# Decode attention plus bilinear GLU: q made as two rows and spread by matmuls with ones, last w_down loads regrouped

## The chip, the cores and the metric

One core of a Trainium2 chip. The metric is device time in microseconds. The kernel before took 377.58 us (median of 3 runs, 377.46 to 377.84).

## What is computed

Two tokens (B = 2), one layer, in float32: the input is normalised, then x + attention(xn) + GLU(xn) is returned.

```python
# D = 512, H = 32 heads of DH = 128, window W = 2048 of SK = 8192 keys, F = 1376
xn = layernorm(x)
q = xn @ wq                                    # 2 x 4096
k, v = k_cache[:, :, SK-W:], v_cache[:, :, SK-W:]   # 2 x 32 x 2048 x 128 each
scores = einsum("bhqd,bhkd->bhqk", q, k) * DH**-0.5
o = einsum("bhqk,bhkd->bhqd", softmax(scores), v)
h = (xn @ w_gate) * (xn @ w_up)
out = x + o.reshape(B, 1, H*DH) @ wo + h @ w_down
```

Every key and value is used once, so the kernel reads some 159 MB to make 1024 numbers.

## The kernel before

The host lays all weights and the used part of the caches out as one stream, in the order in which the kernel wants them; `loads()` lists it. The 32 heads form 11 groups, `GROUPS`, of three heads (the last has two). The stream is cut into steps. A step is one load on the SP queue into one of three big buffers, `step0` to `step2` (13824 floats on each of 128 partitions), or for a few small ones into `extra`. Odd steps bring the keys of a group together with `wq` for the group after it; even steps bring the values and `wo`. Step n goes into the buffer that step n - 3 left, so its issue waits until the readers of that step are through. The last steps are cut small: the values of the last two heads, `wo` for them, and the pieces 2 to 9 of `w_down` (`wd`, each 128 x 512, 256 KB; NFC = 10). Pieces 2 to 9 are three loads on their own.

For a group g:

- `project(g)` makes q on TensorE. `xnb` holds each value of xn repeated over 128 columns, so each of the 8 matmuls (2 tokens by 4 chunks of D) gives q of a token on all 128 partitions at once, in PSUM, in `q_ps[g % 2]`. It is called for g + 1 while VectorE works on group g, behind the first `products` of the group.
- `products(h)` multiplies the keys of a head in place by q on VectorE, reading q from PSUM; `sums(h)` adds over the head dimension. `maxima(g)`, `weights(g)` and `denominators(g)` make the softmax, with the exponentials on ScalarE.
- `weigh(h)` is the product with the values on TensorE; `fold(g)` copies its result to SBUF on ScalarE, `gather(g)` collects it on TensorE and scales it on VectorE into `oT`; `wo(g, ...)` multiplies by wo.

`project_gu`, `gate` and `turn` make the GLU's hidden layer `hT` early. `down(c, ...)` multiplies piece c of w_down. At the end everything is added up in `acc_g`, four column groups of 32 partitions, by `add_groups`, with four matmuls for a piece. VectorE copies `acc_g` to `o_out` and SP stores it.

Each engine runs its instructions in the order in which the program writes them; `Program.emit` sets semaphores between engines and on loads. The order at the end of the program, after the last `fold`, is: `down` of pieces 2 to 4, `gather`, `down` of 5 to 7, `wo`, `down` of 8 and 9, the copy, the store. Nearly all instructions are recorded by the helper in `Engine.__getattr__` and `Program.put`, so in the profile they all carry line 175, and groups are told apart by the names of their tiles. A float32 matmul of the program shows as two matmul and two weight-load instructions.

Of the kernel before, what the change touches and what calls it, by code (L numbers as in the profile page):

```python
# [10 lines left out]
P = 128  # L11
B, D, H, DH, SK, F = 2, 512, 32, 128, 8192, 1376
# [3 lines left out]
NC = D // P  # L16
FB = 4 * P
NFB = -(-F // FB)
NFC = F // P
# [3 lines left out]
HG = 3  # L23
# [10 lines left out]
def loads():  # L34


    def wq(g):
        return ("wq", g, NC * DH * len(GROUPS[g]))

    def k(h):  # L40
        return ("k", h, CK)

    def v(h):
        return ("v", h, CK)

    def wo(h):
        return ("wo", h, CO)

    def wd(lo, hi):
        return [("wd", i, CO) for i in range(lo, hi)]  # L50

    out = [
        (0, "x", [("c", 0, CX), wq(0)]),
        (1, 0, [k(h) for h in GROUPS[0]] + [wq(1)]),
        (2, 1, [(w, 0, NC * F) for w in ("wg", "wu")]),
        (3, 2, [k(h) for h in GROUPS[1]] + [wq(2)]),
    ]
    turn = (1, 0, 2)
    for g in range(NG - 1):
        n = 4 + 2 * g  # L60
        if g < NG - 2:
            out += [(n, turn[n % 3 - 1], [f(h) for f in (v, wo) for h in GROUPS[g]])]
        if g < NG - 3:
            out += [(n + 1, turn[(n + 1) % 3 - 1], [k(h) for h in GROUPS[g + 2]] + [wq(g + 3)])]
        if g == NG - 3:
            out += [(n + 1, turn[(n + 1) % 3 - 1], [k(h) for h in GROUPS[g + 2]]
                     + wd(0, 2) + [wo(h) for h in GROUPS[g + 1]])]
        if g == NG - 2:
            h = GROUPS[g]
            e, f = GROUPS[g + 1]  # L70
            m = turn[(n + 1) % 3 - 1]
            out += [(n, "x", [v(h[0])]), (n + 1, turn[n % 3 - 1], [v(i) for i in h[1:]]),
                    (n + 2, m, [v(e), wo(e), wo(f)]), (n + 2, m, [v(f)]),
                    (n + 2, m, wd(2, 5)), (n + 2, m, wd(5, 8)),
                    (n + 2, m, wd(8, NFC))]
    return out


# [134 lines left out]
def build(nc, stream, x_nat, wd_rest, out):  # L213
    pr = Program(nc)
    pe, dve, act, pool = pr.pe, pr.dve, pr.act, pr.pool
# [9 lines left out]
    xc = pr.sb("xc", [P, B, NC])  # L225
    sq = pr.sb("sq", [P, B, NC])
    xn = pr.sb("xn", [P, NC, B])
    xnb = pr.sb("xnb", [P, NC * B, P])
    cst = pr.sb("cst", [P, CX])
    p_all = pr.sb("p", [P, 2, HG, B, JG, M])  # L230
    s_t = [pr.sb(f"s{i}", [P, 2 * HG, J]) for i in range(2)]
# [14 lines left out]
    q_ps = [pr.ps(f"q{i}", [P, B, FB]) for i in range(2)]  # L246
# [4 lines left out]
    for n, t, fields in loads():  # L251
        tile = buf_x if t == "x" else buf[t]
        c0 = used.get(n, 0)
        for kind, i, w in fields:
            c = used.get(n, 0)
            got[kind, i] = tile[:, c : c + w]
            used[n] = c + w
        c1 = used[n]
        assert c1 <= tile.shape[1], (n, c1)
        src = stream[pos : pos + P * (c1 - c0)].rearrange("(p i) -> p i", p=P)  # L260
        pos += P * (c1 - c0)
        queue.append((n, tile[:, c0:c1], src))
# [21 lines left out]
    for w in (B * NC, 8 * HG, 8 * HG, 2 * NFB, 2):  # L284
# [5 lines left out]
    id2 = cst[:B, cut[4] : cut[5]]  # L290
# [12 lines left out]
        xn, xc.rearrange("p b c -> p c b"),  # L303
        st[:, 3, :].unsqueeze(1).to_broadcast([P, NC, B]), op=ALU.mult,
    )
    dve.tensor_copy(
        xnb, xn.rearrange("p c b -> p (c b)").unsqueeze(2).to_broadcast([P, NC * B, P])
    )

    def project(g):  # L310
        n = DH * len(GROUPS[g])
        w = got["wq", g].rearrange("p (c n) -> p c n", c=NC)
        for b in range(B):
            for c in range(NC):
                pe.matmul(
                    q_ps[g % 2][:, b, 0:n], xnb[:, c * B + b, :], w[:, c, :],
                    start=(c == 0), stop=(c == NC - 1),
                )

    def keys(h):  # L320
        return got["k", h].rearrange("p (b j d) -> p b j d", b=B, j=J)
# [107 lines left out]
    def down(c, add, **kw):  # L429
        add(hT[:, c % 4, c // 4, :], got["wd", c], **kw)  # L430

    def wo(g, add):
        for hh, h in enumerate(GROUPS[g]):
            add(oT[g % 2][:, B * hh : B * hh + B], got["wo", h])
# [10 lines left out]
    def next_up(g):  # L445
        if g + 1 < NG:
            project(g + 1)
        if g == 0:
            project_gu()
        if g == 1:  # L450
            gate()

    project(0)
    for g in range(NG - 1):
        start_group(g, lambda: next_up(g))
# [14 lines left out]
    g = NG - 1  # L470
# [22 lines left out]
    for c in range(5, 8):  # L493
        down(c, add_groups)
    wo(g, add_groups)
    for c in range(8, NFC):
        down(c, add_groups, last=(c == NFC - 1))
    dve.tensor_copy(o_out, acc_g)
    pr.load("SP", out, o_out)
    pr.emit()  # L500
# [2 lines left out]
def laid_out(x):  # L503
# [33 lines left out]
    def field(kind, i):  # L537
# [13 lines left out]
    parts = [  # L551
        np.concatenate([field(kind, i) for kind, i, _ in fields], axis=1).ravel()
        for _, _, fields in loads()
    ]
    return {"stream": np.concatenate(parts), "x": a, "wd_rest": wd[NFC * P :]}
# [27 lines left out]
```

## Time and profile before

| | |
|---|---|
| median of the runs | 377.58 us |
| the profiled execution | 377.47 us |
| its span | 376.2 us |
| mean granted TensorE clock | 0.773 |

The span runs from the first to the last recorded instruction; the rest of the execution's time lies around it. In the page's lists, "PE" is TensorE, "PEld" its weight loads, "DVE" VectorE, "ACT" ScalarE, "SP" the engine that issues the loads. A row of a list of instructions gives the start, the length, the engine, the line, the operation, output <- inputs, shapes, the count, and in brackets how long the engine stood idle before it and what ended that. A row of groups gives the busy time, the mean in ns, and the idle time before. `q1` is the SP queue of loads, `q8` a queue for instructions.

### The profile page before, as it was taken

To read this page: it belongs to the slowest core of one execution; us is meant where nothing else is said; L and a number is where in the kernel's file an instruction comes from. 1 tells how busy PE (TensorE), PEld (TensorE's weight loads), DVE (VectorE), ACT (ScalarE), POOL (GpSimd) and SP (SyncE) were. 2 spreads that over 40 slices of the span, in tenths; PEclk is the share of its full clock that TensorE was granted. 3 is DMA by queue.
4 is the path that set the end of the run, shared out by engine and by line. 5 is a ranking of instruction groups with operands and counts; after the bars stand their busy time and mean duration, and the time that the engine had idled before them with its cause. 6 is when DMAs were issued, how large, how long until landed. Compare 5 with 4: busy or idle time off the path is not lost.

```text
span 376.2 us, 2481 instructions
## 1 busy us (share of the span) xinstructions
PE 224.2 (60%) x1052; PEld 84.2 (22%) x1052; DVE 298.6 (79%) x159; ACT 29.5 (8%) x143; POOL 1.3 (0%) x5
## 2 busy tenths in 40 slices
PE   1764844769178367616927752691775278088287
PEld 1431122124022112302301230230122023012033
DVE  2069989947995995999499499959949986998950
ACT  2000020020001002000100200010020001001010
POOL 1000000000000000000000000000000000000000
PEclk9968858669586958958685895878689588578879
DMA  9999989999899998999999999999999999999995
GB/s 367 400 459 422 459 388 470 390 453 465 383 460 407 447 459 388 460 429 423 459 394 460 423 423 459 400 455 429 417 459 406 443 438 422 422 439 414 427 426 238
DMA packets 4446, 159.70 MB, mean 425 GB/s; under 512 B 498, under 2 KB 626, under 8 KB 1236
## 3 DMA queue, kind: packets, MB, share of 16 engines
q1 hardware_dynamic: 4320, 159.35, 98.4%
q10 hardware_dynamic: 116, 0.20, 0.2%
q8 instruction: 8, 0.13, 0.1%
q14 instruction: 2, 0.02, 0.0%
HBM read 159.49 MB, written 0.07 MB: 424 GB/s over the span
## 4 chain that ended last, share of the span: by engine, by line
DMA 53%; DVE 36%; PE 9%; SPq 0%; issue 0%
DMA step<-in_stream_dram 53%; DVE s L175 18%; DVE step L175 17%; PE acc L175 5%; PE o_ps L175 2%; PE tr L175 1%; PE q L175 1%; SPq L175 0%; DVE dg L175 0%; DVE mt L175 0%; DVE mtt L175 0%; DVE mc L175 0%; DVE o_sb L175 0%; DVE rec L175 0%; DVE oT L175 0%
## 5 line engine op out<-in xcount | busy, mean ns | idle before, releaser
L175 DVE TENSOR_TENSOR step<-step,q 128x4096 f32<-128x4096 f32 x32 | 141.2, 4414 | 43.6 <-DMA step<-in_stream_dram 43.6
L175 DVE TENSOR_REDUCE s<-step 128x32 f32<-128x4096 f32 x32 | 141.4, 4420 | 0.8
L175 PE MATMUL o_ps<-step,p 128*24 128x512 f32 x496 | 76.8, 782 | 98.0 <-DMA step<-in_stream_dram 98.0
L175 PE MATMUL q<-step,xnb 128*128 128x384 f32 (+1 forms) x160 | 57.6, 517 | 5.4 <-DMA step<-in_stream_dram 5.2
L175 PEld LDWEIGHTS o_ps<-step,p 128*24 128x24 f32 x496 | 16.9, 129 | 154.1 <-DMA step<-in_stream_dram 97.4
L175 PE MATMUL acc<-step,oT 128*2 128x512 f32 x54 | 42.3, 948 | 0.0
L175 PEld LDWEIGHTS q<-step,xnb 128*128 128x128 f32 x160 | 32.2, 206 | 26.0 <-DMA step<-in_stream_dram 6.3
L175 ACT COPY o_sb<-o_ps 128x512 f32<-128x512 f32 x12 | 7.0, 584 | 258.0 <-PE o_ps L175 258.0
L175 ACT ACTIVATE p<-s,nm 128x16 f32<-128x16 f32 x64 | 18.8, 294 | 76.5 <-DVE nm L175 76.5
L175 PE MATMUL tr<-dg,ones 128*128 128x24 f32 (+1 forms) x22 | 5.9, 351 | 23.2 <-DVE dg L175 23.2
L175 PE MATMUL tr<-cst,o_sb 128*128 128x6 f32 (+1 forms) x96 | 12.7, 256 | 7.0 <-ACT o_sb L175 7.0
L175 PEld LDWEIGHTS tr<-cst,o_sb 128*128 128x128 f32 x96 | 11.6, 191 | 17.2 <-ACT o_sb L175 14.9
L175 PE MATMUL o_ps<-step,xn 128*2 128x512 f32 (+1 forms) x48 | 9.9, 741 | 5.0 <-DMA step<-in_stream_dram 5.0
L175 ACT ACTIVATION_READ_ACCUMULATOR p<-s,nm 128x1 f32 x64 | 11.9, 187 | 0.0
L175 PEld LDWEIGHTS acc<-step,oT 128*2 128x2 f32 x54 | 5.2, 108 | 24.3 <-issue 23.9
L175 PEld LDWEIGHTS tr<-dg,ones 128*128 128x128 f32 x22 | 4.6, 261 | 25.8 <-DVE dg L175 24.9
L175 DVE TENSOR_REDUCE nm<-tr 128x6 f32<-128x24 f32 (+1 forms) x11 | 2.0, 183 | 8.5 <-PE tr L175 8.5
L175 PE MATMUL q<-extra,xnb 128*128 128x384 f32 x16 | 7.4, 631 | 1.5 <-DVE xnb L175 1.5
L175 DVE TENSOR_TENSOR oT<-tr,rec 128x6 f32<-128x6 f32 (+1 forms) x11 | 1.7, 157 | 7.0 <-PE tr L175 7.0
L175 PEld LDWEIGHTS tr<-rs,ones 128*128 128x128 f32 x22 | 3.7, 213 | 14.4 <-issue 11.7
L175 PE MATMUL tr<-rs,ones 128*128 128x6 f32 (+1 forms) x22 | 4.7, 286 | 2.4 <-ACT p L175 2.2
L175 PE MATMUL tr<-st,mean_w 128*128 128x2 f32 x4 | 1.2, 363 | 7.2 <-DVE st L175 7.2
(44 smaller groups left out, 40.9 us busy)
## 6 DMA issues: line engine op xcount, KB each, us to landing
step<-in_stream_dram SPq DMA_DIRECT2D x18, 6912.0 KB, 23.0
step<-in_stream_dram SPq DMA_DIRECT2D x1, 6656.0 KB, 33.3
step<-in_stream_dram SPq DMA_DIRECT2D x1, 5504.0 KB, 33.6
step<-in_stream_dram SPq DMA_DIRECT2D x1, 5376.0 KB, 34.3
step<-in_stream_dram SPq DMA_DIRECT2D x1, 4096.0 KB, 26.0
step<-in_stream_dram SPq DMA_DIRECT2D x1, 2560.0 KB, 28.4
extra<-in_stream_dram SPq DMA_DIRECT2D x1, 2048.0 KB, 38.7
step<-in_stream_dram SPq DMA_DIRECT2D x1, 2048.0 KB, 31.6
```

What stands on the lines that cost most here:

```text
L175: ins = getattr(e, method)(*args, **kw)
```

## The change

q of a group is first made as two rows (one for each token) by four matmuls with xn itself as the stationary tile, into the second bank of `q_ps`; ScalarE copies the two rows to SBUF; two matmuls with `one_b`, a 2 x 128 tile with ones in the row of one token, spread each row over the 128 partitions. `xnb` goes, and with it its copy on VectorE; `one_b` is made by a smaller one. The three last loads bring pieces 2 to 4, 5 to 8 and 9 of w_down, in place of 2 to 4, 5 to 7 and 8 to 9.

```diff
@@ loads
-                    (n + 2, m, wd(2, 5)), (n + 2, m, wd(5, 8)),
-                    (n + 2, m, wd(8, NFC))]
+                    (n + 2, m, wd(2, 5)), (n + 2, m, wd(5, 9)),
+                    (n + 2, m, wd(9, NFC))]
@@ build
-    xnb = pr.sb("xnb", [P, NC * B, P])
+    one_b = pr.sb("one_b", [B, B, P])
+    q_sb = [pr.sb(f"q_sb{i}", [B, HG * DH]) for i in range(2)]
...
-    dve.tensor_copy(
-        xnb, xn.rearrange("p c b -> p (c b)").unsqueeze(2).to_broadcast([P, NC * B, P])
-    )
+    dve.tensor_copy(one_b, id2.unsqueeze(2).to_broadcast([B, B, P]))

     def project(g):
         n = DH * len(GROUPS[g])
         w = got["wq", g].rearrange("p (c n) -> p c n", c=NC)
+        q2 = q_ps[g % 2][0:B, B - 1, 0:n]
+        for c in range(NC):
+            pe.matmul(q2, xn[:, c, :], w[:, c, :], start=(c == 0), stop=(c == NC - 1))
+        act.copy(q_sb[g % 2][:, 0:n], q2)
         for b in range(B):
-            for c in range(NC):
-                pe.matmul(
-                    q_ps[g % 2][:, b, 0:n], xnb[:, c * B + b, :], w[:, c, :],
-                    start=(c == 0), stop=(c == NC - 1),
-                )
+            pe.matmul(
+                q_ps[g % 2][:, b, 0:n], one_b[:, b, :], q_sb[g % 2][:, 0:n],
+                start=True, stop=True,
+            )
...
-    for c in range(8, NFC):
-        down(c, add_groups, last=(c == NFC - 1))
+    down(8, add_groups)
+    down(9, add_groups, last=True)
```

The order of the matmuls at the end stays as it was: `down` of 5 to 7, `wo`, `down` of 8, `down` of 9.

## The prediction

> **What bounds the kernel now.** I read the page's busy shares and slices first, then its queues and its chain, then the chain in order of time, then the last ten microseconds instruction by instruction.
>
> ```profile
> PE 224.2 (60%) x1052; PEld 84.2 (22%) x1052; DVE 298.6 (79%) x159; ACT 29.5 (8%) x143; POOL 1.3 (0%) x5
> ...
> DMA  9999989999899998999999999999999999999995
> ...
> q1 hardware_dynamic: 4320, 159.35, 98.4%
> ...
> q8 instruction: 8, 0.13, 0.1%
> ...
> HBM read 159.49 MB, written 0.07 MB: 424 GB/s over the span
> ...
> DMA 53%; DVE 36%; PE 9%; SPq 0%; issue 0%
> ```
>
> The one load queue keeps the 16 DMA engines occupied for 98.4% of the span; no compute engine is above 79%. The chain gives the DMA only 53% because it walks through VectorE wherever a buffer is freed, but the slices show no stretch in which the transfers stand still before the last one. So the end is set by the bytes, by the few microseconds before the first and by those after the last, unless a load is issued so late that the queue runs empty. How far is that?
>
> ```profile
> DMA to landing us min/median/max: 21.1/31.1/49.5
> ...
> 52.00:68.00 16.00, 8.40 (x18) 4.62 (x18) 15.96 (x6) 1.07 (x6) 0.00 (x0) 0.71 1.02 442
> ```
>
> The first row is for all 27 loads into the step buffers, the second a busy stretch whose last column is GB/s. A full load is 6912 KB, 7.08 MB, and takes 16.0 us at 442 GB/s. Even the load with the shortest time from issue to landing, 21.1 us, was therefore issued some 5 us before the transfers ahead of it were through. Nothing starves.
>
> What is left is the tail:
>
> ```profile
> 308.30 21.93 DMA step<-in_stream_dram
> 330.23 0.04 issue
> 330.27 7.61 PE o_ps L175 x48
> 337.89 0.27 SPq L175
> 338.15 0.04 issue
> 338.20 34.10 DMA step<-in_stream_dram
> 372.30 0.04 issue
> 372.34 1.88 PE q L175 x56
> 374.22 0.02 issue
> 374.24 0.29 DVE o_out L175
> ```
>
> ```profile
> 371.23 1.05 PE L175 MATMUL tr<-cst,o_sb 128*128 128x4 f32 x8
> 372.32 0.16 DVE L175 TENSOR_TENSOR oT<-tr,rec 128x4 f32<-128x4 f32 x1 [6.22 <-PE tr L175]
> 372.34 0.84 PE L175 MATMUL q<-step,hT 128*2 128x128 f32 x24
> 372.99 0.62 PE L175 MATMUL q<-step,oT 128*2 128x128 f32 x16
> 373.56 0.33 PEld L175 LDWEIGHTS q<-step,hT 128*2 128x2 f32 x16 [0.24 <-DMA step<-in_stream_dram]
> 373.56 0.62 PE L175 MATMUL q<-step,hT 128*2 128x128 f32 x16
> ```
>
> The first view is the chain (start, length, what), the second the instructions in order of time. The load of pieces 5 to 7 of w_down lands at 372.30; TensorE then does 24 matmul instructions for them, 16 for wo of the last group, waits 0.24 us for pieces 8 and 9, which land about 373.54, does 16 more, and VectorE copies the sums out. From 372.30 to the copy the program is no longer bound by transfers alone but by a landing plus the TensorE work queued behind it.
>
> **The change part by part: q.** Before, project(g) is 8 matmuls over a 128-wide stationary tile; each shows as two instructions.
>
> ```profile
> 22.29 8.01 PE L175 MATMUL q<-step,xnb 128*128 128x384 f32 x16 [5.04 <-DMA step<-in_stream_dram]
> ...
> 151.12 4.81 PEld L175 LDWEIGHTS q<-step,xnb 128*128 128x128 f32 x16 [0.19 <-DMA step<-in_stream_dram]
> 151.12 5.43 PE L175 MATMUL q<-step,xnb 128*128 128x384 f32 x16
> 155.44 0.19 DVE L175 RECIPROCAL rec<-tr 128x6 f32<-128x6 f32 x1
> ...
> ACT o_sb L175 <- PE o_ps L175: 258.0, 11, 27.1
> ...
> PE o_ps L175 <- DMA step<-in_stream_dram: 103.0, 11, 12.3
> ...
> L175 DVE TENSOR_TENSOR step<-step,q 128x4096 f32<-128x4096 f32 x32 | 141.2, 4414 | 43.6 <-DMA step<-in_stream_dram 43.6
> L175 DVE TENSOR_REDUCE s<-step 128x32 f32<-128x4096 f32 x32 | 141.4, 4420 | 0.8
> ```
>
> The first row is the slow case at the start, 8.01/16 = 0.50 us an instruction; the next two are the usual one: sixteen loads in 4.81 us are 0.30 us each, with 0.62 us of trailing time. After, there are 4 + 2 matmuls, 12 instructions: 3.6 us if each keeps its 0.30, plus the 0.62, plus one hop to ScalarE and back. The trace has no copy of 2x384 from PSUM; the nearest rows bound it, 0.59 us for 128x512 above the tail and 0.26 us for the 128x2 square root:
>
> ```profile
> 8.40 0.26 ACT L175 ACTIVATE st<-tr,eps 128x2 f32<-128x2 f32 x1 [5.38 <-PE tr L175]
> ...
> 370.57 0.59 ACT L175 COPY o_sb<-o_ps 128x512 f32<-128x512 f32 x1 [5.33 <-PE o_ps L175]
> 371.23 0.97 PEld L175 LDWEIGHTS tr<-cst,o_sb 128*128 128x128 f32 x8 [0.22 <-ACT o_sb L175]
> ```
>
> I take 0.55, since the free size of 384 is nearer to 512, and 0.07 for the way back (370.57 + 0.59 to 371.23). The matmuls before the hop must also drain, another 0.62 at most. That makes 4.8 to 5.4 us against 5.43: a gain of 0 to 0.6 us of TensorE per group. If all 12 ran at the slow 0.50, it would be 6.0 + 1.8, a loss of 2.4 us per group. Neither reaches the end. The new wait stands in TensorE's queue ahead of weigh(g-1), which itself waits for the V load: TensorE stood 103.0 us for these landings in 11 waits, over 9 us each. ScalarE's copy sits between the weights of the group before and fold(g-1), for which ScalarE idles 258.0 us. The consumer of q, the products of the next group, comes a whole group of VectorE work later. SP's load over the finished keys waits for project(g+1) as well as for the last sums of group g, but three products and three sums of 4.42 us end some 26 us after the keys land, and the projection about 5. I cost it at 0. Without that cover it would be at most 10 groups times the figures above, minus 6 to plus 24 us, but it takes a projection over four times as long to lift the cover.
>
> **The start.** xnb, 128x1024, gives way to one_b, 2x256, and the first projection waits for xn alone.
>
> ```profile
> 9.10 0.69 DVE L175 COPY xnb<-xn 128x1024 f32<-128x1024 f32 x1
> 9.85 7.41 PE L175 MATMUL q<-extra,xnb 128*128 128x384 f32 x16 [1.48 <-DVE xnb L175]
> ...
> 22.35 4.42 DVE L175 TENSOR_TENSOR step<-step,q 128x4096 f32<-128x4096 f32 x1 [12.55 <-DMA step<-in_stream_dram]
> ```
>
> Up to 0.7 us is saved at 9.1 us and the first projection can shorten, but the first products wait for the keys until 22.29 in any case, 5.0 us after q is there. Cost 0, hidden behind that load; without it, a gain of 1 to 3 us.
>
> **The tail.** The same three loads follow each other, with 3, 4 and 1 pieces for 3, 3 and 2. Total bytes, queue order and number of issues stay, so the last landing stays at 373.54. The middle load now lands one piece later. Two pieces took 373.54 - 372.30 = 1.24 us, one is 0.62, so it lands at 372.92. All 56 instructions stand behind that landing, because down(5) to down(7) come first in TensorE's order and need it. Their pace: 24 instructions from 372.34 to 372.99, 0.027 us each; the last 16 take 0.62, of which 0.43 is pace and 0.19 trails. Hence 372.92 + 0.04 + 56 x 0.027 + 0.19 = 374.66 for the end of TensorE, where it was 373.56 + 0.62 = 374.18. The wait for the last piece disappears (TensorE reaches down(9) at about 374.3, after 373.54), but it had cost only 0.24. **Sum: +0.5 us.** Bounds: if every instruction takes the 0.62/16 = 0.039 us of the last group instead, 372.96 + 2.17 = 375.13, +0.95; if the middle load's landing is not held up at all, the end is the last landing plus 8 instructions, 373.56 + 0.62 - 0.22 = 373.96, which is -0.2.
>
> The Trainium skill speaks against the last load: its page "DMA: Bandwidth & Descriptors", section Bandwidth, asks for DMAs of at least 1 MiB and fits each as about 2.0 us plus its bytes; by that, an estimate from the page, a 256 KB load standing alone would land 2.6 us after the one before it. The trace does not bear this out for queued loads, since 512 KB landed 1.24 us after its predecessor, with nothing left for a fixed part.
>
> The profiled execution is 377.47 us with a span of 376.2, and lies 0.11 below the median of 377.58. So 377.47 + 0.5 is 378.0, and beside the median 378.1; I say **378.0**. A difference of 0.2%, 0.75 us, is about what a measurement of this kernel can tell from no change, and the forecast lies below it.
>
> **The rivals.**
> *A fetched block of code delays the last transfers (slower).* q8 is the instruction queue: 8 transfers of 0.13 MB together, 16 KB each, on the same 16 engines. At 425/16, 26.6 GB/s for one engine, such a block holds its engine for 0.62 us, and up to 1.2 if a packet of the stream shares the time. A load is complete when its slowest engine is, so one block on an engine is paid already, but two on the same engine would add up. TensorE has 2104 matmul and weight-load instructions; 88 go (22 matmuls of 4), so the blocks move to later moments, and one that fell into the idle time before the tail moves into it. Price 0.6 to 1.2 on top of 0.5: 378.6 to 379.3. It decides once a block falls on an engine that has had one. For it: the count hardly drops. Against: 8 blocks on 16 engines need not meet. The Trainium skill ("Runtime: NRT & Kernel Launch", Instruction fetch mechanics) has refills of 256 instructions in 16 KB and calls them mostly hidden; the size agrees with 0.13 MB in 8.
> *The last load pays for itself (slower).* The lone 64 KB store took 1.6 us to land:
>
> ```profile
> out_dram<-o_out SPq DMA_DIRECT2D x1, 64.0 KB, 1.6
> ```
>
> A 256 KB load that did not overlap its neighbour would take some 2.05 us from 372.92, land at 374.97 and end TensorE 0.45 later: +1.2, 378.7. The landing distance of 1.24 us speaks against it.
> *The tail shortens as the smaller last load suggests (faster).* The -0.2 above, 377.3; it needs the middle load to land by 372.3 with a third more bytes.
> *Less code frees the last engine (faster).* 2016 instructions are 7.9 blocks instead of 8.2; if the block that goes had held the last engine, -0.6 to -1.2 beside the +0.5, 376.9 to 377.9.
> *The new projection starves the queue.* It would have to hold up a load by more than 5 us; I see no place.
>
> **How the numbers follow.** Forecast 0.70, code 0.12, lone last load 0.05, shorter tail 0.06, freed engine 0.05, starving 0.02. The forecast's own range is 377.7 to 378.4, with a seventh of its chance above 0.2%. Slower: 0.10 + 0.11 + 0.05 + 0.02 = 0.28. Faster: 0.03 of the freed engine and 0.04 for a tail or start that I have undervalued, 0.07. The rest, 0.65, is within 0.2%. The range for 8 in 10 goes from 377.3, the shorter tail, to 378.8, past the lone load and half of the code rival.
>
> **What would show it.** After: the chain's last TensorE piece starts near 372.9 instead of 372.3 with no wait before down(9); the copy out starts near 374.7; q1 stays near 98%; project takes 12 instructions per group, its time shifts TensorE's idle and nothing else; the smallest time from issue to landing stays near 21 us. A last landing other than 373.5, or any slice of transfers that empties, would prove me wrong; a shift of the last landing by a microsecond with unchanged issues would point to the code blocks.

## The result, and the profile after

The changed kernel takes 380.87 us (median of 11 runs, 379.48 to 381.66) where the kernel before takes 377.84 (11 runs beside it, 377.46 to 379.79). The ratio is 1.0065, with a 95% interval of 1.0046 to 1.0084: 2.5 us slower (the two medians lie 3.0 apart), where +0.5 was predicted and the range ended at 378.8. The executions of most kernels here scatter over 2 us or more, so ratios carry the comparison; the last experiments follow the scatter.

The profiled execution took 381.47 us, with a span of 380.2. Its page answers to the one of before:

```profile
PE 214.8 (57%) x1008; PEld 64.2 (17%) x1008; DVE 298.2 (78%) x159; ACT 34.5 (9%) x154; POOL 1.3 (0%) x5
...
q1 hardware_dynamic: 4320, 159.35, 97.6%
...
q8 instruction: 8, 0.13, 0.1%
...
DMA 47%; DVE 40%; PE 11%; ACT 1%; issue 0%; SPq 0%; DVEq 0%
```

TensorE works 9.4 us less, and the number of code blocks is the same. But the loads fill 97.6% of the span instead of 98.4, and ScalarE, which was not in the chain, has a percent of it. The chain in order of time tells where; these are pieces of it from the second group (start, length, what), where the chain of before has VectorE's work alone:

```profile
52.59 0.59 PE tr L175 x2
53.18 5.01 PE q L175 x8
58.22 0.47 ACT q_sb L175
58.69 0.49 ACT o_sb L175
59.20 0.69 DVE o_sb L175
```

And this is the same place in the lists of instructions, of the kernel before and then of the one after, each with the load that SP issues over the keys of this group when VectorE is through with them:

```profile
52.50 0.56 ACT L175 COPY o_sb<-o_ps 128x512 f32<-128x512 f32 x1
52.65 0.60 PE L175 MATMUL tr<-rs,ones 128*128 128x6 f32 x2 [2.16 <-ACT p L175]
53.10 7.95 PE L175 MATMUL q<-step,xnb 128*128 128x384 f32 x16
56.08 0.65 DVE L175 TENSOR_TENSOR o_sb<-o_sb,o_ps 128x512 f32<-128x512 f32 x1
56.64 4.41 DVE L175 TENSOR_REDUCE s<-step 128x32 f32<-128x4096 f32 x1
...
78.64 0.33 SPq L175 DMA_DIRECT2D step<-in_stream_dram  x1
```

```profile
55.91 0.19 DVE L175 RECIPROCAL rec<-tr 128x6 f32<-128x6 f32 x1
58.22 0.47 ACT L175 COPY q_sb<-q 2x384 f32<-2x384 f32 x1 [5.68 <-PE q L175]
58.59 0.57 ACT L175 COPY o_sb<-o_ps 128x512 f32<-128x512 f32 x1
59.20 0.69 DVE L175 TENSOR_TENSOR o_sb<-o_sb,o_ps 128x512 f32<-128x512 f32 x1 [3.10 <-ACT o_sb L175]
59.80 4.41 DVE L175 TENSOR_REDUCE s<-step 128x32 f32<-128x4096 f32 x1
...
81.80 0.33 SPq L175 DMA_DIRECT2D step<-in_stream_dram  x1
```

In the second group `next_up` calls `project(2)` and then `gate()`, whose ScalarE copy of `o_ps` feeds a VectorE product. Before, that copy ran at 52.50, right behind the exponentials, and VectorE never noticed it. Now it stands in ScalarE's queue behind the copy of the two q rows, which waits for the four matmuls of the first part of `project(2)`, which stand behind the denominators on TensorE. VectorE reaches the gate's product at 56.1 and finds nothing: 3.10 us of idling in the one engine whose sums free the key buffers. It is the only place where VectorE waits for such a copy in this profile.

What it does to the transfers, in stretches of 2 us (last column GB/s), of the kernel before and then of the one after:

```profile
84.00:86.00 2.00, 2.00 (x7) 0.54 (x5) 0.00 (x0) 0.00 (x0) 0.00 (x0) 0.61 1.02 442
118.00:120.00 2.00, 2.00 (x5) 0.28 (x3) 1.58 (x1) 0.00 (x0) 0.00 (x0) 0.58 1.02 442
```

```profile
82.00:84.00 2.00, 1.14 (x3) 0.58 (x4) 0.88 (x5) 0.27 (x2) 0.00 (x0) 0.50 1.02 387
84.00:86.00 2.00, 2.00 (x4) 0.33 (x3) 0.00 (x0) 1.59 (x12) 0.00 (x0) 0.50 0.83 332
116.00:118.00 2.00, 0.68 (x3) 0.59 (x4) 1.18 (x7) 0.00 (x0) 0.00 (x0) 0.50 1.21 415
118.00:120.00 2.00, 2.00 (x3) 0.25 (x2) 0.17 (x1) 1.80 (x12) 0.00 (x0) 0.50 0.67 276
```

The load over the keys of group 1 (it brings the values of that group) is issued at 81.80 us instead of 78.64, and the one over the keys of group 2 at 116.27 instead of 113.14, and behind each the queue runs short. Against a steady 442 GB/s these four stretches lack 358 GB/s for 2 us, 0.72 MB, 1.6 us of the stream. That is not made up: the keys of the last group land 2.0 us later, as VectorE's first product with them shows, before and after:

```profile
342.97 4.42 DVE L175 TENSOR_TENSOR step<-step,q 128x4096 f32<-128x4096 f32 x1 [0.78 <-DMA step<-in_stream_dram]
```

```profile
344.97 4.42 DVE L175 TENSOR_TENSOR step<-step,q 128x4096 f32<-128x4096 f32 x1 [0.92 <-DMA step<-in_stream_dram]
```

From there to the copy of the result the execution of before needs 374.24 - 342.97 = 31.27 us, this one 378.01 - 344.97 = 33.04. Of the 4.0 us between the two spans, 2.0 are the late stream and 1.8 the tail.

These 1.8 us are not the predicted half microsecond of the regrouped loads. The load of four pieces is issued at 344.90 and lands 30.0 us later, at 374.9, the forecast 372.9 plus the 2.0 of the stream. TensorE comes to these pieces only at 376.24, and its own queue is the chain's end:

```profile
370.23 4.37 PE o_ps L175 x32
...
376.31 1.68 PE q L175 x56
```

The same 32 value products took 3.71 us in the profile of before. From 363 to 368 and from 368 to 374 us the granted clock was 0.80 and 0.72 here, and 1.00 in both stretches there. The last experiments come back to this.

### The profile page after: what moved, and what is told of

Same layout as the page of the kernel before. It is cut to its first block, busy times and chain, and to the rows that moved or that the text cites. A ratio compares the mean times of both kernels' runs of the same rounds, so it can differ in the third digit from the quotient of the medians.

```text
span 380.2 us, 2404 instructions
## 1 busy us (share of the span) xinstructions
PE 214.8 (57%) x1008; PEld 64.2 (17%) x1008; DVE 298.2 (78%) x159; ACT 34.5 (9%) x154; POOL 1.3 (0%) x5
## 3 DMA queue, kind: packets, MB, share of 16 engines
q1 hardware_dynamic: 4320, 159.35, 97.6%
## 4 chain that ended last, share of the span: by engine, by line
DMA 47%; DVE 40%; PE 11%; ACT 1%; issue 0%; SPq 0%; DVEq 0%
DMA step<-in_stream_dram 47%; DVE s L175 20%; DVE step L175 18%; PE acc L175 5%; PE o_ps L175 3%; PE q L175 2%; PE tr L175 2%; ACT p L175 0%; ACT o_sb L175 0%; DVE dg L175 0%; DVE mtt L175 0%; DVE mt L175 0%; DVE mc L175 0%; DVE o_sb L175 0%; DVE oT L175 0%
## 5 line engine op out<-in xcount | busy, mean ns | idle before, releaser
L175 PE MATMUL o_ps<-step,p 128*24 128x512 f32 x496 | 77.6, 790 | 97.3 <-DMA step<-in_stream_dram 97.3
L175 PE MATMUL acc<-step,oT 128*2 128x512 f32 x54 | 43.3, 968 | 0.0
L175 PE MATMUL q<-step,xn 128*2 128x384 f32 (+1 forms) x80 | 31.3, 542 | 6.6 <-DMA step<-in_stream_dram 6.5
L175 PE MATMUL q<-q_sb,one_b 2*128 2x384 f32 (+1 forms) x44 | 16.6, 497 | 6.0 <-ACT q_sb L175 6.0
L175 ACT COPY q_sb<-q 2x384 f32<-2x384 f32 (+1 forms) x11 | 5.0, 459 | 72.2 <-PE q L175 72.2
L175 PEld LDWEIGHTS q<-step,xn 128*2 128x2 f32 x80 | 6.5, 91 | 24.5 <-issue 16.1
L175 PEld LDWEIGHTS q<-q_sb,one_b 2*128 2x128 f32 x44 | 7.3, 184 | 17.7 <-ACT q_sb L175 14.9
```

Source lines behind the costliest of these rows:

```text
L175: ins = getattr(e, method)(*args, **kw)
```

## The experiments

Theory W: the gate's copy behind q's copy in ScalarE's queue holds up VectorE, and the V loads with it. Rivals: T, the regrouped last loads; C, a block of code falling twice on one DMA engine.

**The gate's copy first.** The changed kernel with two statements of `next_up` exchanged:

```diff
     def next_up(g):
+        if g == 1:
+            gate()
         if g + 1 < NG:
             project(g + 1)
         if g == 0:
             project_gu()
-        if g == 1:
-            gate()
```

> The changed kernel with gate() called before project(2) in the second group, so that ScalarE copies o_ps for the gate before it waits for the two q rows. Theory W (the copy of the gate stands behind q_sb's copy in ScalarE's queue, VectorE waits 3.1 us for it, and two V loads are issued 3.1 us late and leave the transfers idle): VectorE's gate product starts at about 56.1 instead of 59.2 with no wait for ScalarE, the seventh full load is issued at about 78.6 instead of 81.8, the dips at 84 to 86 and 118 to 120 us are gone, and the time is 377.8 to 378.4, some 2.5 us under the changed kernel. Rival T (the regrouped last loads cost it): still 380 to 381. Rival C (a block of code falls twice on one DMA engine): still 379 to 381.

378.52 us, median of 12 (377.92 to 379.57), ratio to before 1.0005 (0.9988 to 1.0022). The median lies 0.1 above what was expected. The loss is gone with the wait, in the list of instructions:

```profile
52.39 0.56 ACT L175 COPY o_sb<-o_ps 128x512 f32<-128x512 f32 x1
55.97 0.65 DVE L175 TENSOR_TENSOR o_sb<-o_sb,o_ps 128x512 f32<-128x512 f32 x1
57.73 0.47 ACT L175 COPY q_sb<-q 2x384 f32<-2x384 f32 x1 [4.78 <-PE q L175]
...
78.54 0.33 SPq L175 DMA_DIRECT2D step<-in_stream_dram  x1
```

The V load is issued at 78.54 again, the stretch from 84 to 86 us is back at 442 GB/s and the one from 118 to 120 at 419, and the last group's first product starts at 342.96. T falls, since the regrouped loads are in this kernel. The eight code blocks are still there too, which speaks against C; the kernels below that lose as much without the new projection settle it.

**The two parts of the change alone.** First the new q with the old grouping of the loads (3, 3 and 2), then the old q with the new one (3, 4 and 1); each is the diff of the change without the other part.

> The changed kernel with the last loads as they were before (3, 3 and 2 pieces). Theory W: VectorE still waits 3.1 us for ScalarE at 56 us and the time stays 2 to 3 us above before, 379.5 to 380.9. Rival T: back to 377.6 to 378. Rival C: 379 to 381 without any gap in the transfers near 85 and 118 us.

380.38 us (12 runs, 378.71 to 382.43), ratio 1.0055 (1.003 to 1.008). The q part makes the loss by itself; in the profiled execution, the shortest of the twelve, VectorE's wait was 2.20 us.

> The kernel before with the last loads of 3, 4 and 1 pieces alone. Theory W: no wait of VectorE at 56 us, only the tail moves, by the predicted +0.5: 377.8 to 378.5. Rival T: 379.5 to 381. Rival C: as before, 377.5 to 378.

378.18 us (12 runs, 377.99 to 379.86), ratio 0.9998 (0.9981 to 1.0016). No loss that can be told from noise by the ratio. The times hint at the predicted one: the eight shorter ones lie from 377.99 to 378.28, and the shorter ones of before, fourteen of thirty, from 377.42 to 377.71. In the profile the tail is the predicted one, instruction by instruction:

```profile
373.13 0.84 PE L175 MATMUL q<-step,hT 128*2 128x128 f32 x24 [0.64 <-DMA step<-in_stream_dram]
373.79 0.62 PE L175 MATMUL q<-step,oT 128*2 128x128 f32 x16
374.22 0.62 PE L175 MATMUL q<-step,hT 128*2 128x128 f32 x16
374.91 0.29 DVE L175 COPY o_out<-q 128x128 f32<-128x128 f32 x1 [2.22 <-PE q L175]
```

TensorE now waits for the load of four pieces, then runs 56 instructions without a break. It ends at 374.84, which is 0.66 after 374.18; 0.2 of that is the stream, which in this execution is 0.2 late already at the last keys (343.17).

**The wait without the change.** The kernel before, with one copy ahead of the gate's, of two rows of q to a tile that nobody reads:

```diff
         if g == 1:
+            act.copy(q_junk, q_ps[0][0:B, 0, 0 : HG * DH])
             gate()
```

> The kernel before with one ScalarE copy of two rows of q (2x384, to a tile that nobody reads) put ahead of the gate's copy in the second group; it waits for the first four matmuls of project(2). Theory W: this wait alone makes the loss: the gate product starts 2 to 4 us late, the seventh full load is issued at about 81 to 82, the transfers dip near 85 and 118 us, and the time is 1.5 to 3 us above before. Rivals T and C: unchanged, 377.5 to 378.

381.24 us (7 runs, 380.25 to 382.85), ratio 1.0069 (1.0044 to 1.0095), as much as the whole change. The old projection, `xnb` and the old loads are all in place; only ScalarE's queue differs, and VectorE waits 3.41 us:

```profile
58.48 0.47 ACT L175 COPY q_junk<-q 2x384 f32<-2x384 f32 x1 [6.00 <-PE q L175]
58.85 0.57 ACT L175 COPY o_sb<-o_ps 128x512 f32<-128x512 f32 x1
59.46 0.69 DVE L175 TENSOR_TENSOR o_sb<-o_sb,o_ps 128x512 f32<-128x512 f32 x1 [3.41 <-ACT o_sb L175]
```

**How much delay the loads bear.** The kernel before with 2, 4 or 6 memsets of 128x512 on VectorE behind the gate's product. ScalarE and TensorE are left alone.

```diff
         if g == 1:
             gate()
+            for _ in range(6):          # 2, 4, 6
+                dve.memset(late, 0.0)
```

> The kernel before with two memsets of 128x512 on VectorE behind the gate's product, about 1 us of delay and nothing else: no wait of ScalarE or TensorE. Theory M (the V loads are issued with a margin of 1 to 2 us, not the 5 us of the prediction): no gap in the transfers, 377.5 to 378.3, as before. Theory of the prediction (5 us): the same.

> As the one with two memsets, with four: about 2 us of delay. Theory M: at the edge, 0.3 to 1.2 us over before, a first dip of the transfers at 118 to 120 us. The prediction's 5 us: as before. Theory Q (what costs is ScalarE's or TensorE's work being late, not VectorE's): as before.

> As the one with two memsets, with six: about 3 us, as much as the wait in the changed kernel. Theory M: 1.5 to 3 us over before, dips at 84 to 86 and 118 to 120 us. The prediction's 5 us, and theory Q: as before.

The memsets take 0.48 us each and wait 0.17 for one another, so the delays are a little longer than meant. From the start of the gate's product to the start of the sums it was 0.56 us before; with the memsets 1.76, 3.08 and 4.39. The kernel before, measured beside them, has a median of 377.70 (27 runs):

| | VectorE later by | median (runs) | ratio to before (95%) | the same in us, of 377.7 |
|---|---|---|---|---|
| 2 memsets | 1.20 us | 378.51 (12) | 1.0008 (0.9984 to 1.0032) | 0.3 |
| 4 memsets | 2.52 us | 380.60 (9) | 1.0057 (1.0033 to 1.0080) | 2.2 |
| 6 memsets | 3.83 us | 381.79 (7) | 1.0083 (1.0052 to 1.0114) | 3.1 |
| the change | 3.10 us | 380.87 (11) | 1.0065 (1.0046 to 1.0084) | 2.5 |

VectorE's lateness alone makes a loss, and most of each delay comes through: each loss is its delay less 0.3 to 0.9 us. An interval leaves a loss uncertain by about 1 us either way; taken together, the four leave a margin of 0 to 1.3 us for the V loads, an estimate, where the prediction had 5. My own expectation of 1 to 2 us was too large as well: four memsets were to cost 0.3 to 1.2 us and cost 2.2. The profiled executions say much the same: with two, four and six memsets the last group's first product starts at 344.15, 344.82 and 345.31, so the stream is 1.2, 1.9 and 2.3 us late, the delay less 0 to 1.5 us. With six memsets the transfers fall to less than a third in one stretch:

```profile
84.00:86.00 2.00, 2.00 (x5) 0.50 (x5) 0.18 (x1) 1.46 (x10) 0.00 (x0) 0.50 0.42 138
```

**What the new projection is worth.** q's new way with the gate's copy first and the old loads.

> The changed kernel with gate() ahead of project(2) and the last loads as before (3, 3 and 2 pieces): q's new way with its wait out of VectorE's path. Theory W: 377.4 to 378.1, the kernel before to within 0.2%. If the new projection has a cost of its own that the gate's order does not explain: 378.5 or more.

379.15 us (12 runs, 377.45 to 380.51), ratio 1.0010 (0.9988 to 1.0033). The ratio says no difference. The median lies 1.45 us above that of before, but the twelve times fall into two groups: five from 377.45 to 377.58, seven from 379.10 to 380.51, and before has both too (16 of 27 runs up to 377.97, 11 from 379.02). So the median hangs on how many fall where. At 379.15 it lies above what theory W expected, where I had put a cost of the new projection itself; the five short times, as short as any of before, speak against such a cost. The profiled execution is one of the long ones, and its transfers are not late: the keys of the last group are multiplied from 342.86, earlier than in the profile of before, which is one of the short ones. What differs is the granted clock (the last figure but two of a row). First the profile of before, then this one:

```profile
357.00:363.00 6.00, 5.41 (x32) 1.21 (x32) 4.48 (x5) 0.00 (x0) 0.00 (x0) 0.58 0.99 421
363.00:368.00 5.00, 4.26 (x60) 2.67 (x60) 1.11 (x4) 1.77 (x9) 0.00 (x0) 1.00 0.97 409
368.00:374.00 6.00, 5.95 (x112) 3.16 (x104) 0.16 (x1) 0.59 (x1) 0.00 (x0) 1.00 0.70 285
```

```profile
357.00:363.00 6.00, 5.51 (x28) 1.27 (x32) 4.38 (x5) 0.00 (x0) 0.00 (x0) 0.50 0.97 416
363.00:368.00 5.00, 4.26 (x56) 2.58 (x52) 1.11 (x4) 1.76 (x9) 0.00 (x0) 0.84 0.98 413
368.00:374.00 6.00, 5.94 (x66) 2.15 (x58) 0.00 (x0) 0.59 (x1) 0.00 (x0) 0.82 0.68 275
```

From 368 to 374 us TensorE got through 112 matmul instructions at full clock and 66 at 0.82, where it also came in later. The queue of value products then ends after the last landing and sets the end. That all long executions are of this kind is theory P; so far it rests on these profiles.

**Taking TensorE's queue out of the tail.** The load of the values of heads 28 and 29 is cut in two, so that head 28 can be weighed earlier, in the kernel before and in the last kernel.

```diff
-(n + 1, turn[n % 3 - 1], [v(i) for i in h[1:]]),
+(n + 1, turn[n % 3 - 1], [v(h[1])]), (n + 1, turn[n % 3 - 1], [v(h[2])]),
```

> The kernel before with the load of the values of heads 28 and 29 (4096 KB) cut into two loads of one head each, nothing else. Theory P (the longer executions of every kernel here, some 1.7 us above the shorter ones, are those in which TensorE's clock is granted at half in the last 15 us, so that its queue of value products and not the last landing sets the end): head 28's 16 matmul instructions run at about 353 instead of 357.5, in TensorE's idle time, the tail has 1.9 to 3.4 us of slack more, and the times are 377.4 to 378.0 in nearly all runs, median 377.6. Rival (the longer executions come from the transfers): still two groups near 377.5 and 379.3.

> q's new way with gate() ahead of project(2), the last loads as before (3, 3, 2), and the load of heads 28 and 29 in two. Theory P: 377.4 to 378.0 in nearly all runs, the same as the split kernel with the old projection, so the new projection itself costs and brings nothing. Rival: two groups near 377.5 and 379.4, as without the split.

378.25 us (11 runs, 377.72 to 378.38; ratio 1.0002, 0.9986 to 1.0019) and 378.28 us (11 runs, 377.54 to 378.58; 0.9994, 0.9970 to 1.0018), beside a before of 377.67 (21 runs, 377.44 to 380.87). The long executions are gone, as theory P has it: no run of the 22 is above 378.6. (The last kernel with the split still has two groups, but closer ones: 377.54 to 377.79 and 378.28 to 378.58.) So it is TensorE's queue that makes them long; that the clock decides which ones is shown only by the profiles above. Head 28's products moved into the idle time as expected, here in the kernel before with the split:

```profile
352.81 1.92 PE L175 MATMUL o_ps<-step,p 128*24 128x512 f32 x16 [2.79 <-DMA step<-in_stream_dram]
357.71 2.73 PE L175 MATMUL o_ps<-step,p 128*24 128x512 f32 x16 [2.98 <-DMA step<-in_stream_dram]
```

But the typical run is at 378.3, not 377.6 as expected: in the profile of the same kernel (0.50 granted from 363 to 368 us) TensorE's tail still ends 0.8 us after the one in the profile of before. The split narrows the scatter and wins nothing on the median, so no version here beats the kernel before by more than a measurement can tell.

## Why the prediction was wrong

- **The step that failed** is in the q part: "ScalarE's copy sits between the weights of the group before and fold(g-1), for which ScalarE idles 258.0 us", costed at 0. No other copy shows a wait of VectorE for it. For the one in the second group it doesn't hold: `gate()` puts its own ScalarE copy there, between the two that I named, and VectorE's next instruction waits 3.10 us for it, so that the V load goes out 3.16 us late and the stream ends up 2.0 us late. I named what was queued behind the new wait on TensorE, and took a sum of idle time for the answer on ScalarE. The copy was free until the instruction ahead of it in the queue could wait.
- **The cover was mis-sized too.** That every load was "issued some 5 us before the transfers ahead of it were through" came from the shortest landing, 21.1 us, less 16.0 us of bytes. The 21.1 us belong to the first load of keys, issued at 1.15; the two V loads took 23.4 and 21.6. The delays put the margin at 0 to 1.3 us. What the subtraction leaves out is the time from the issue until every free one of the sixteen DMA engines has a packet of the load. The packet records of the changed kernel show it: the load issued at 81.80 reaches the last idle engine at 84.96, the one issued at 116.27 at 117.99, so 3.2 and 1.7 us later. In the trace of before the first engines are through with the earlier loads 4.7 us after the issue at 78.64 and 2.9 us after the one at 113.14. So the second place has a margin of 1.2 us at most, as an estimate, and with two memsets only that one runs short (359 GB/s from 114 to 116 us, 442 from 84 to 86). With a true 5 us even the 3.1 us wait would have cost nothing.
- **The starving queue** was the rival that came true. I gave it 0.02, "I see no place", and held that it would need a delay of more than 5 us. Its place was the gate.
- **The tail** was right in its mechanism. Forecast: four pieces land at 372.92, TensorE ends at 374.66. Where the stream wasn't late and TensorE's queue in time, in the kernel with the gate's copy first, the landing is at 372.9 and the end at 374.02 + 0.62 = 374.64 (its chain's last TensorE piece is below). The regrouping does cost about half a microsecond there, but the ratio of the kernel with the regrouping alone, 0.9998, cannot be told from 1. In the profile of the changed kernel this term did not decide the end.

```profile
372.93 1.75 PE q L175 x56
```

- **The lone last load** fell: in the kernel with the gate's copy first the load of four pieces lands at 343.86 + 29.0 = 372.9 and the one of a single piece at 345.57 + 27.9 = 373.5, 0.6 us apart, which is its share of the bytes. The Trainium skill's fixed 2.0 us for each DMA ("DMA: Bandwidth & Descriptors", section "Anatomy of one DMA — SWDGE (gpsimd) path", where the prediction named Bandwidth) is a fit for DMAs issued by GpSimd; it does not add up for these loads, which SP issues and which are queued behind one another.
- **The code blocks** are eight before and after (0.13 MB), also in the kernels without loss; so their number explains nothing of the 2.5 us.
- **TensorE's saving and the start** had no effect on the end, as costed. The saving was larger than thought: TensorE is busy 9.4 us less, where 0 to 0.6 a group had been taken, the hop to ScalarE included. The first products start at 22.28 where it was 22.35.

## What to carry to other kernels

An instruction that begins to wait changes what everything behind it on its engine costs, so list the neighbours at every place where the new instruction is emitted, the one special group included; the sum of an engine's idle time says nothing of that place. A margin worked out as time to landing less bytes over bandwidth was far too large here, since it takes no account of the time from issue to the first packets: where a schedule leans on it, delay the issuing engine by known amounts and find the point at which the stream breaks. A stall of 2.5 to 4 us in an engine off the bound came through for three quarters or more, because this stream never pauses and so a gap in it was not made up.

## What the runs showed of the hardware that was not expected

The granted TensorE clock moves between 0.5 and 1 within an execution (0.58, 1.00 and 1.00 against 0.50, 0.84 and 0.82 in the same three stretches of the tail), and two kernels whose last keys landed at the same time to 0.1 us ended 1.9 us apart (copies of the result at 374.24 and 376.16), with TensorE's queue setting the later end. A kernel that is bound by its loads can have a tail that is bound by TensorE's clock. Cutting one load so that TensorE's queue empties earlier narrowed the scatter of the kernel before from 377.44 to 380.87 down to 377.72 to 378.38. What decides the phase of the clock in an execution stays open.

A large load is not on the sixteen DMA engines when it is issued: in the changed kernel 1.7 and 3.2 us passed until the last idle engine had its first packet.
